# Batch 0's scores in two banks, the embeddings' place, the routing's arithmetic, and the planner's clock

## The chip, the cores and the metric

The kernel runs on one core of a Trainium2 chip. The metric is the device time of one execution in microseconds; the median of three runs is given. A core has TensorE (PE, matrix products; PEld is its weight load), VectorE (DVE), ScalarE (ACT), GpSimd (POOL) and SyncE (SP, which here only issues transfers). Each takes its instructions in the order in which they were put into its queue.

## The reference

Three layers follow one another. `x` is 8 batches x 8 heads x 512 x 64, `state` 8 x 8 x 32 x 64; there are 8 x (512 + 32) = 4608 tokens of 512 numbers, in 36 tiles of 128.

```python
a = softmax(x @ state.T / 8);  xread = a @ state          # per batch and head
a2 = softmax(state @ x.T / 8); sread = a2 @ x
x = concat([xread, sread])                                # 4608 x 512 tokens
x = square(maximum(x @ w_in, 0)) @ w_out                  # 512 -> 2048 -> 512
xn = x / (norm(x) + 1e-6); en = emb / (norm(emb) + 1e-6)
logits = xn @ en.T / tau                                  # 8 experts
e = argmax(logits); gate = softmax(logits)[e]
out = gate * (maximum(x @ w1[e], 0) @ w2[e])              # 512 -> 1024 -> 512
```

## The kernel before

Nearly all products are made of float16 pairs: a number is split into a high and a low half, and a product is three float16 products (high x high, high x low, low x high). The weights of the first dense layer arrive as 64-bit numbers, in 16 blocks (8 of `w_in`, 8 of `w_out`); ACT and DVE turn each into float32 bits (`to_f32`, lines 864 to 896: a scaling on ACT, line 882, and three integer steps on DVE, lines 885, 887 and 894), ACT squares it (lines 911, 967) for a scale, and both split it.

The order of all instructions is written before the kernel runs, by a planner in the same file (`Plan`, line 103). Each piece of work is a generator, a thread with a priority. It yields `(engine, duration)` before it issues instructions, or an event or a buffer ring to wait for. `run` (line 150) picks again and again the thread that can start earliest by the plan's own clock, the smaller priority number first, and lets it issue. So the durations that threads yield set only the order within the queues; on the chip, semaphores make each instruction wait for its inputs. `dma` (line 137) gives the plan's arrival time of a load. Everything else follows from these orders, so any edit of a duration or a priority can move instructions in all queues.

The stages run into one another. In the first 130 us the weights are prepared, batch 0 goes through attention and the first tokens through the dense layer in float32 (`first_attention` to `first_state_w`, lines 560 to 665; line 1412). Batches 1 to 7 follow (`attention`, line 448), with the dense layer in pairs (`up1`, `down1`, lines 1325 and 1367) and the routing of each tile. From about 700 us on the experts' layer runs (`moe2`, line 1773).

What the change touches:

- Batch 0's scores. `first_attention` takes one tile `S` of two PSUM banks; `first_scores(t)` (line 591) makes 16 float32 products for each half `t` as soon as that half of `x` is there; `weigher` (line 508) then makes the softmax of the half: maximum (line 519), subtraction (521), exponential on ACT (528), sum (530), normalisation (532 to 536), a float16 split (540, 542) and a turned read by DMA on SP's queue (549). `weights` (line 976) asks for the weight blocks from the fifth on only after both turned reads were asked for (`AHEAD`, `ev("asked", t)`).
- `embeddings` (line 1134) normalises the eight expert embeddings: 3 small DVE steps, a float32 product with ones (line 1146), 19 small DVE steps (1149 to 1159, with `rsqrt`). It waits for the weights' scale and for `prepare`, which loads `tsb` (tau) and `emf` (the embeddings) on SP's queue (lines 1817 to 1830).
- Routing. `route_tile` (line 1166) squares a finished tile, makes a power-of-two scale from the sum (`pow2`, line 294), splits, turns and multiplies with the embeddings. `route_group` (line 1205) works for four tiles at once (the last group has two): scale, largest logit, one-hot `oh`, and the running count `cum` of tokens per expert, one DVE addition per tile (line 1246); one product with a triangle of ones and one with ones of `cum` (lines 1253, 1254) give each token's place in its expert's list, to which the expert's base is added (1259).

Of the kernel before, what the change touches and what calls it, by code (L numbers as in the profile page):

```python
# [10 lines left out]
F32 = mybir.dt.float32  # L11
F16 = mybir.dt.float16
# [10 lines left out]
NE, FE = 8, 1024  # L23
# [34 lines left out]
RECS = 6  # L58
MARG = 1.75
# [43 lines left out]
class Plan:  # L103
# [10 lines left out]
    MARGIN = MARG  # L114

    def __init__(self):
        self.free = dict.fromkeys(("pe", "act", "dve", "pool", "sp"), 0.0)
        self.dma_free = 0.0
        self.threads = []
        self.cur = None  # L120
# [28 lines left out]

    def run(self):  # L150
        while self.threads:
            best = None
            for th in self.threads:
                r = th[3]
                if isinstance(r, Ev):
                    if r.time is not None:
                        th[2] = max(th[2], r.time)
                        self._advance(th)
                        break
                elif isinstance(r, Slots):  # L160
                    if r.ready():
                        th[2] = max(th[2], r.take())
                        self._advance(th)
                        break
                else:
                    dep = r[2] if len(r) > 2 else th[2]
                    if r[0] == "pe" and 1.3 <= th[1] < 5:
                        dep += self.MARGIN
                    key = (max(dep, self.free[r[0]]), th[1])
                    if best is None or key < best[0]:  # L170
                        best = (key, th, dep)
            else:
                assert best is not None, "threads wait for each other"
                (start, _), th, dep = best
                eng, dur = th[3][0], th[3][1]
                self.free[eng] = start + dur
                th[2] = start + dur + self.LAT
                self._advance(th)
# [57 lines left out]
def tiny(k):  # L236
    return "dve", TINY * k
# [7 lines left out]
def moe_kernel(  # L245
# [47 lines left out]

    def pow2(s, inv, v, K):

        m = small.tile([128, 4], F32, name="p2m")[:, :v.shape[1]]
        V.tensor_scalar(out=m.bitcast(I32), in0=v.bitcast(I32), scalar1=0x7F000000, scalar2=1,
                        op0=ALU.bitwise_and, op1=ALU.logical_shift_right)
        V.tensor_scalar(out=s.bitcast(I32), in0=m.bitcast(I32), scalar1=-1.0, scalar2=float(K << 23),
                        op0=ALU.mult, op1=ALU.add)  # L300
        V.tensor_scalar(out=inv.bitcast(I32), in0=m.bitcast(I32), scalar1=float((254 - K) << 23), scalar2=None,  # L301
                        op0=ALU.add)
# [74 lines left out]
    cum = const.tile([128, NT + 1, NE], F16, name="cum")  # L377
    nc.gpsimd.memset(cum[:, 0, :], 0.0)
# [21 lines left out]
    def ev(*key):  # L400
        return evs.setdefault(key, Ev(plan))
# [46 lines left out]
    def attention(b):  # L448
# [56 lines left out]
        w = weigher(b, Sp, xh, xl, scl, 0, 32)  # L505
        yield from w

    def weigher(b, Sp, xh, xl, scl, m0, m1):

        ms, n = slice(m0, m1), NS * (m1 - m0)  # L510
        S4 = Sp.rearrange("p a (h n) -> p (a h) n", n=NS)[:, ms]
# [10 lines left out]
        ev("S read", b, m1).set()  # L522
        if m1 == 32:
            if m0:
                yield ev("S read", b, m0)
            s_slots.release()
# [33 lines left out]
    def first_attention():  # L560

        yield ev("st", 0)
        stt = st_t.pop(0)
        yield xhl_slots
        xh, xl = halves_tile()
        ss = small.tile([128, 3], F32, name="ss")
        yield act(256)
        nc.scalar.activation(out=xl.bitcast(BF16)[:, :, :64], in_=stt, func=AF.Square, accum_out=ss[:, 2:3])
        yield t_slots
        p = ps_t.tile([128, 512], F32, name="t")  # L570
        yield "pe", 0.2
        mm(p[:, 2:3], lhsT=one32, rhs=ss[:, 2:3], start=True, stop=True)
        mm(p[:, 256:512], lhsT=oneb, rhs=xl.bitcast(BF16)[:, :, :64], start=True, stop=True)
        yield s_slots
        Sp = ps_s.tile([128, 4, 256], F32, name="S")
        for t in range(2):
            plan.add(first_scores(t, Sp, xh, xl, stt), 0.4 + 0.1 * t)
        plan.add(first_scale(ss, stt), 0.95)
        v = small.tile([128, 2], F32, name="sv")[:, 0:1]
        yield tiny(4)  # L580
        V.tensor_scalar(out=v, in0=p[:, 2:3], scalar1=FLOOR, scalar2=None, op0=ALU.max)
        pow2(sx[:, 1:2], isx[:, 1:2], v, 204)
        yield sth_slots
        sthl = att.tile([128, 2, 4, 64], F16, name="sthl")
        stf = sthl.rearrange("p a c n -> p (a c n)").bitcast(F32).rearrange("p (c n) -> p c n", c=4)
        yield dve2(256)
        V.tensor_scalar(out=stf, in0=stt, scalar1=sx[:, 1:2], scalar2=float(2.0 ** -14), op0=ALU.mult, op1=ALU.mult)
        plan.add(first_state_w(stf), 0.6)
        plan.add(group_bound(0, p), 0.7)

    def first_scores(t, Sp, xh, xl, stt):
        yield ev("first x", t)
        xf = xf_t[0, 0]
        yield "pe", 2.0
        for sb in (2 * t, 2 * t + 1):
            for c in range(4):
                mm(Sp[:, sb, c * 64:c * 64 + 64], lhsT=xf[:, c, sb * 128:sb * 128 + 128], rhs=stt[:, c, :],
                   start=True, stop=True)
        ev("scored", t).set()
        yield from weigher(0, Sp, xh, xl, eighth, 16 * t, 16 * t + 16)  # L600
# [533 lines left out]
    def embeddings():  # L1134
        yield ev("wo scale")
        yield ev("prepared")
        yield "dve", 3.0
        V.reciprocal(out=itau, in_=tsb)
        V.tensor_scalar(out=itau, in0=itau, scalar1=float(2.0 ** -14), scalar2=None, op0=ALU.mult)
# [7 lines left out]
        yield tiny(20)  # L1147
# [3 lines left out]
        y = small.tile([128, NE], F32, name="eny", bufs=1)  # L1151
        rsqrt(y, v, NE)
        V.tensor_tensor(out=y, in0=y, in1=v, op=ALU.mult)
# [12 lines left out]
    def route_tile(i, ps, k_h, rc, st):  # L1166
# [8 lines left out]
        yield tiny(4)  # L1175
        f2 = st["f2"][:, j:j + 1]
        V.tensor_scalar(out=f2, in0=f2, scalar1=FLOOR, scalar2=None, op0=ALU.max)
        s2 = small.tile([128, 1], F32, name="s2")
        pow2(s2, st["is2"][:, j:j + 1], f2, 204)
# [25 lines left out]
    def route_group(i0, m, recs, k_r, st):  # L1205
# [15 lines left out]
        yield tiny(12)  # L1221
        V.tensor_tensor(out=ui, in0=u1[:, i0:i0 + m], in1=is2, op=ALU.mult)
        rsqrt(y, f2, m)
        yield tiny(9)
        V.tensor_tensor(out=L, in0=f2, in1=y, op=ALU.mult)
        V.tensor_tensor(out=L, in0=L, in1=u1[:, i0:i0 + m], op=ALU.mult)
        V.tensor_scalar(out=L, in0=L, scalar1=1e-6, scalar2=None, op0=ALU.add)
# [4 lines left out]
        V.tensor_tensor(out=eq, in0=l2, in1=bc(lm), op=ALU.is_equal)  # L1232
# [224 lines left out]
    def list_of(which, J, tiles):  # L1457
# [7 lines left out]
        mm(pc[:, 0:NE], lhsT=one16, rhs=cum[:, tiles, :], start=True, stop=True)  # L1465
# [13 lines left out]
        V.tensor_copy(tot, pc[:, 0:NE])  # L1479
# [337 lines left out]
    def prepare():  # L1817

        yield ev("w_in asked")
        yield from load(cs, cst, 1 << 17)  # L1820
        yield from load(cs16, cst16, 1 << 16)
        yield from load(rid, rowid, 1 << 15)
        yield from load(tsb, tau.to_broadcast([128, 1]), 512)
        t = yield from load(emf, embT, 1 << 14)
        yield "pool", 1.0, t
        dz = mg.tile([128, REC], F32, name="rec0", bufs=1)
        nc.gpsimd.memset(dz, 0.0)
        nc.gpsimd.tensor_copy(dz[:, 513:514].bitcast(I32), rid[:, NT:NT + 1])
        yield from load(rec_d[NOREC:NOREC + 1, :], dz[0:1, :].bitcast(I32), 2048)
        ev("prepared").set()  # L1830

    def start():
        plan.add(first_attention(), PRIO_A0)
        yield from load_st(0)
# [7 lines left out]
        plan.add(embeddings(), 3)  # L1842
# [50 lines left out]
```

## Time and profile before

| | |
|---|---|
| median of 3 runs | 1088.94 us (1087.68 to 1089.35) |
| the profiled execution | 1089.88 us, span 1088.1 us from the first to the last instruction |
| mean granted clock of PE | 0.984 |
| PE busy | 1039.9 us (96% of the span), 10657 products |
| DVE busy | 684.6 us (63%) |
| ACT busy | 588.2 us (54%) |
| POOL busy | 124.3 us (11%) |
| DMA | 211.74 MB, mean 195 GB/s |

Busy times are shares of the span. [...] In a row of the timeline the part in brackets is the time for which the engine stood idle just before, and what ended it. In a row of waits stand who waited, for whom, the total, the number of times and the longest.

### The profile page before, as it was taken

How to read it: one execution, taken by the hardware profiler on the slowest of the kernel's cores; microseconds unless marked ns; L12 is line 12 of the kernel's file. 1: busy time of each engine (PE TensorE's matmuls, PEld its weight loads, DVE VectorE, ACT ScalarE, POOL GpSimd, SP SyncE). 2: the span in 40 equal slices, each digit the busy share in tenths (PEclk: the TensorE clock that was granted, in tenths of full speed). 3: DMA queues.
4: the chain of work that ended last, by engine and by line, in shares of the span. 5: the costliest groups of instructions: out<-in, count | busy, mean ns of one | idle time of the engine just before them, and what ended most of it. 6: DMA issues, size and time to landing. Idle time of an engine off the chain costs nothing. (4 is left out here: it accounts for less than half of the span.)

```text
span 1088.1 us, 26339 instructions
## 1 busy us (share of the span) xinstructions
PE 1039.9 (96%) x10657; PEld 672.2 (62%) x10657; DVE 684.6 (63%) x1787; ACT 588.2 (54%) x976; POOL 124.3 (11%) x149
## 2 busy tenths in 40 slices
PE   4679999999999999999999999999999999999997
PEld 3345446565656566565555666677677777767774
DVE  5788798868878778887797784466322323222222
ACT  4778779787887988887787984211110101111110
POOL 0000000200101001002002020312122121212111
PEclk8799999999999999999999999999999999999999
DMA  6873144874875565887559587753898777694691
GB/s 216 288 248 110 60 97 146 233 209 133 242 226 150 153 181 173 233 210 217 166 162 262 194 262 246 218 138 80 277 285 166 195 226 219 169 292 141 182 311 69
DMA packets 161311, 211.74 MB, mean 195 GB/s; under 512 B 112225, under 2 KB 114529, under 8 KB 155938
## 3 DMA queue, kind: packets, MB, share of 16 engines
q1 hardware_dynamic: 152866, 182.94, 58.2%
q0 software_dynamic: 8320, 27.08, 8.2%
q8 instruction: 85, 1.39, 0.5%
q14 instruction: 40, 0.33, 0.1%
HBM read 257.92 MB, written 51.68 MB: 285 GB/s over the span
## 5 line engine op out<-in xcount | busy, mean ns | idle before, releaser
L1699 ACT ACTIVATE r<-u 128x512 f32<-128x512 f32 x70 | 41.8, 597 | 319.5 <-PE u L1745 288.7
L1433 PE MATMUL d<-wo_t,g 128*128 128x512 f16 x480 | 182.1, 379 | 1.0 <-DVE g L1319 1.0
L1435 PE MATMUL d<-wo_t,g 128*128 128x512 f16 x480 | 182.1, 379 | 0.2
L1434 PE MATMUL d<-wo_t,g 128*128 128x512 f16 x480 | 182.1, 379 | 0.0
L1349 PE MATMUL u<-aT,sw 128*128 128x256 f16 x512 | 141.3, 276 | 9.7 <-ACT r L1302 7.6
L1351 PE MATMUL u<-aT,sw 128*128 128x256 f16 x512 | 141.0, 275 | 0.2 <-DVE sw L316 0.2
L1350 PE MATMUL u<-aT,sw 128*128 128x256 f16 x512 | 141.0, 275 | 0.0
L1702 DVE CAST hh<-r 128x512 f16<-128x512 f32 x70 | 29.9, 428 | 127.8 <-ACT r L1699 126.3
L1302 ACT ACTIVATE r<-u,cg 128x512 f32<-128x512 f32 x120 | 81.5, 680 | 47.9 <-PE u L1351 27.2
L1713 DVE TENSOR_SCALAR o<-d,rec,wo_t 128x512 f32<-128x512 f32 x35 | 28.3, 810 | 111.0 <-PE d L1768 108.5
L1275 POOL DMA_INDIRECT rec_d<-rec,pi x34 | 38.5, 1132 | 519.9 <-DVE is L301 140.8
L1768 PEld LDWEIGHTS <-hh 128*128 128x128 f16 (+1 forms) x688 | 54.7, 103 | 57.6 <-issue 1.3
L1321 DVE TENSOR_TENSOR g<-r,g 128x512 f16<-128x512 f32 x120 | 82.2, 688 | 7.5 <-ACT r L1316 5.9
L1435 PEld LDWEIGHTS <-g 128*128 128x128 f16 x480 | 46.9, 98 | 57.7 <-DVE g L1321 1.2
L1743 PE MATMUL u<-xes,stage 128*128 128x128 f16 x448 | 75.9, 219 | 0.0
L1745 PE MATMUL u<-xes,stage 128*128 128x128 f16 x448 | 75.9, 219 | 0.0
L1744 PE MATMUL u<-xes,stage 128*128 128x128 f16 x448 | 75.9, 219 | 0.0
L1433 PEld LDWEIGHTS <-g 128*128 128x128 f16 x480 | 47.2, 98 | 46.3 <-DVE g L1319 1.9
L1316 ACT ACTIVATE r<-r 128x512 f32<-128x512 f32 x120 | 74.5, 626 | 1.4
L1434 PEld LDWEIGHTS <-g 128*128 128x128 f16 x480 | 46.9, 98 | 44.2
L1743 PE MATMUL u<-xes,xx 128*128 128x128 f16 x416 | 70.5, 220 | 0.0
L1744 PE MATMUL u<-xes,xx 128*128 128x128 f16 x416 | 70.4, 219 | 0.0
(338 smaller groups left out, 2637.7 us busy)
## 6 DMA issues: line engine op xcount, KB each, us to landing
w_d<-he SPq DMA_DIRECT2D x128, 256.0 KB
g<-w_d SPq DMA_DIRECT2D x16, 2048.0 KB
wo_t<-w_d SPq DMA_DIRECT2D x16, 2048.0 KB
stage<-w_d SPq DMA_DIRECT2D x14, 2048.0 KB
he<-w_d SPq DMA_DIRECT2D x14, 2048.0 KB
xx<-w_d SPq DMA_DIRECT2D x13, 2048.0 KB
sw<-w_d SPq DMA_DIRECT2D x13, 2048.0 KB
stage<-in_w_dram SPq DMA_DIRECT2D x20, 1024.0 KB
```

Of the source, the lines that this page charges most:

```text
L1302: nc.scalar.activation(out=r, in_=ps, func=AF.Relu, scale=cg[:, g:g + 1] if u >= F32U else cgq[:, c:c + 1])
L1316: nc.scalar.activation(out=r, in_=r, func=AF.Square)
L1321: V.tensor_tensor(out=gl, in0=r, in1=gh, op=ALU.subtract)
L1349: mm(o, lhsT=hl[:, i, 0, fs], rhs=aT[:, i, :], start=i == 0, stop=False)
L1350: mm(o, lhsT=hl[:, i, 0, fs], rhs=aT[:, 2 + i, :], start=False, stop=False)
L1351: mm(o, lhsT=hl[:, i, 1, fs], rhs=aT[:, i, :], start=False, stop=i == 1)
L1433: mm(ps, lhsT=g_h[:, f, ts], rhs=w[:, 0, :], start=f == 0, stop=False)
L1434: mm(ps, lhsT=g_h[:, f, ts], rhs=w[:, 1, :], start=False, stop=False)
L1435: mm(ps, lhsT=g_l[:, f, ts], rhs=w[:, 0, :], start=False, stop=f == KF - 1)
L1743: mm(p[:, j, xs], lhsT=w[:, 0, k, fs], rhs=xe[:, k, xs], start=k == 0, stop=False)
L1744: mm(p[:, j, xs], lhsT=w[:, 0, k, fs], rhs=xe[:, 4 + k, xs], start=False, stop=False)
L1745: mm(p[:, j, xs], lhsT=w[:, 1, k, fs], rhs=xe[:, k, xs], start=False, stop=k == 3)
```

## The change

The plan's clock: PE's durations pass through `slowed`. The plan's time is cut into equal stretches; in a stretch PE counts at half speed unless the one before was used for enough of its length. The first load counts as arriving 1.2 us later. Batch 0's scores: each half gets a PSUM bank of its own, from the ring of the dense layer's `u` tiles, and gives it back once its half is read; `weigher` gets a function to call for that. PE gets five products of ones with ones (`warm`) at the start and four more ahead of the scores. The embeddings' two loads go to ACT's queue, and `embeddings` is started at once, with priority 0.9 instead of 3, in smaller pieces. Routing: the clamp and the inverse scale are made once per group instead of once per tile, steps are fused, the counts of a group are one reduction over `tally` (a ring of four groups, which holds each group's starting counts and its one-hots; 36 times the expert's number is put into the first group's starting counts, so that the product with ones carries the base); the product with ones becomes one per tile of the group. `pow2` is cut into `half`, `power` and `inverse` with the same arithmetic; `list_of` takes the base off again.

```diff
+TALLY = 4
...
-        self.dma_free = 0.0
+        self.dma_free = 1.2
+        self.windows = {}
...
+    def slowed(self, start, dur):
+
+        t, left = start, dur
+        while left > 1e-9:
+            w = int(t / self.WINDOW)
+            before = self.windows.get(w - 1, (0.0, 0.5))
...
+            step = min(left / rate, (w + 1) * self.WINDOW - t + 1e-6)
+            self.windows[w] = self.windows.get(w, (0.0, rate))[0] + step, rate
+            t, left = t + step, left - step * rate
+        return t - start
...
+                if eng == "pe":
+                    dur = self.slowed(start, dur)
...
-        ev("S read", b, m1).set()
-        if m1 == 32:
-            if m0:
-                yield ev("S read", b, m0)
-            s_slots.release()
+        read()
...
+        yield d_slots
+        idle, k_d = ps_d.tile([128, 512], F32, name="d"), d_slots.last()
+
+        def warm(n):
+            yield "pe", 0.25 * n
+            for _ in range(n):
+                mm(idle.rearrange("p (a n) -> p a n", a=4), lhsT=oneb, rhs=oneb.unsqueeze(1).to_broadcast([128, 4, 128]),
+                   start=True, stop=True)
+
+        yield from warm(5)
...
-        yield s_slots
-        Sp = ps_s.tile([128, 4, 256], F32, name="S")
+        at = plan.now()
+        yield from warm(4)
+        d_slots.release(k_d)
+        plan.cur[2] = at
         for t in range(2):
-            plan.add(first_scores(t, Sp, xh, xl, stt), 0.4 + 0.1 * t)
-        plan.add(first_scale(ss, stt), 0.95)
+            plan.add(first_scores(t, xh, xl, stt), 0.4 + 0.1 * t)
+        plan.add(first_scale(ss, stt), 1.2)
...
-    def first_scores(t, Sp, xh, xl, stt):
+    def first_scores(t, xh, xl, stt):
         yield ev("first x", t)
         xf = xf_t[0, 0]
-        yield "pe", 2.0
-        for sb in (2 * t, 2 * t + 1):
+        at = plan.now()
+        yield u_slots
+        plan.cur[2] = max(at, plan.now())
+        Sp, k_h = ps_u.tile([128, 512], F32, name="u").rearrange("p (a n) -> p a n", a=2), u_slots.last()
+        yield "pe", 1.9
+        for a in range(2):
+            sb = 2 * t + a
             for c in range(4):
-                mm(Sp[:, sb, c * 64:c * 64 + 64], lhsT=xf[:, c, sb * 128:sb * 128 + 128], rhs=stt[:, c, :],
+                mm(Sp[:, a, c * 64:c * 64 + 64], lhsT=xf[:, c, sb * 128:sb * 128 + 128], rhs=stt[:, c, :],
                    start=True, stop=True)
         ev("scored", t).set()
-        yield from weigher(0, Sp, xh, xl, eighth, 16 * t, 16 * t + 16)
+        S4 = Sp.rearrange("p a (h n) -> p (a h) n", n=NS)
+        yield from weigher(0, S4, xh, xl, eighth, 16 * t, 16 * t + 16, lambda: u_slots.release(k_h))
...
-        yield ev("wo scale")
-        yield ev("prepared")
-        yield "dve", 3.0
+        yield "act", 1.0
+        nc.scalar.dma_start(emf, embT)
+        nc.scalar.dma_start(tsb, tau.to_broadcast([128, 1]))
+        plan.cur[2] += 2.5
+        yield tiny(1)
         V.reciprocal(out=itau, in_=tsb)
+        yield tiny(2)
...
-        yield tiny(4)
-        f2 = st["f2"][:, j:j + 1]
-        V.tensor_scalar(out=f2, in0=f2, scalar1=FLOOR, scalar2=None, op0=ALU.max)
+        yield tiny(2)
         s2 = small.tile([128, 1], F32, name="s2")
-        pow2(s2, st["is2"][:, j:j + 1], f2, 204)
+        half(st["is2"][:, j:j + 1], st["f2"][:, j:j + 1])
+        power(s2, st["is2"][:, j:j + 1], 204)
...
-        yield tiny(12)
-        V.tensor_tensor(out=ui, in0=u1[:, i0:i0 + m], in1=is2, op=ALU.mult)
+        g, u1s = i0 // 4, u1[:, i0:i0 + m]
+        yield tiny(14)
+        inverse(is2, is2, 204)
+        V.tensor_tensor(out=ui, in0=u1s, in1=is2, op=ALU.mult)
+        V.tensor_scalar(out=f2, in0=f2, scalar1=FLOOR, scalar2=None, op0=ALU.max)
         rsqrt(y, f2, m)
-        yield tiny(9)
+        yield tiny(7)
         V.tensor_tensor(out=L, in0=f2, in1=y, op=ALU.mult)
-        V.tensor_tensor(out=L, in0=L, in1=u1[:, i0:i0 + m], op=ALU.mult)
-        V.tensor_scalar(out=L, in0=L, scalar1=1e-6, scalar2=None, op0=ALU.add)
+        if g < B:
+            V.tensor_scalar(out=L, in0=L, scalar1=u1s[:, 0:1], scalar2=1e-6, op0=ALU.mult, op1=ALU.add)
+        else:
+            V.tensor_tensor(out=L, in0=L, in1=u1s, op=ALU.mult)
+            V.tensor_scalar(out=L, in0=L, scalar1=1e-6, scalar2=None, op0=ALU.add)
...
-        V.tensor_tensor(out=eq, in0=l2, in1=bc(lm), op=ALU.is_equal)
...
-        oh = small.tile([128, 4, NE], F16, name="oh")[:, :m]
-        yield tiny(3 + m) + (at,)
-        V.tensor_tensor(out=eq, in0=eq, in1=revb, op=ALU.mult)
+        if g >= TALLY:
+            yield ev("ranked", g - TALLY)
+        turn_ = tally[:, g % TALLY]
+        oh = turn_[:, 1:1 + m, :]
+        yield tiny(4) + (at,)
+        V.scalar_tensor_tensor(out=eq, in0=l2, scalar=0.0, in1=revb, op0=ALU.is_equal, op1=ALU.mult)
         V.tensor_reduce(out=em, in_=eq, axis=X, op=ALU.max)
         V.tensor_tensor(out=oh, in0=revb, in1=bc(em), op=ALU.is_equal)
-        for j in range(m):
-            V.tensor_tensor(out=cum[:, i0 + j + 1, :], in0=cum[:, i0 + j, :], in1=oh[:, j, :], op=ALU.add)
+        if i0 == 0:
+            V.tensor_scalar(out=turn_[:, 0, :], in0=eix, scalar1=float(NTOK // 128), scalar2=None, op0=ALU.mult)
+        at = plan.now()
+        if i0 + m < NT:
+            after = tally[:, (g + 1) % TALLY, 0, :]
+            if g + 1 >= TALLY:
+                yield ev("ranked", g + 1 - TALLY)
+        else:
+            after = seen[:, 1, :]
+        yield tiny(1) + (at,)
+        with nc.allow_low_precision("counts up to 272"):
+            V.tensor_reduce(out=after, in_=turn_[:, 0:m + 1, :].rearrange("p a e -> p e a"), axis=X, op=ALU.add)
+        if i0 + m == SEEN:
+            V.tensor_copy(seen[:, 0, :], after)
...
-        yield "pe", 0.06
+        yield "pe", 0.15
         mm(pk[:, 0:m * NE], lhsT=ltri16, rhs=oh.rearrange("p a e -> p (a e)"), start=True, stop=False)
-        mm(pk[:, 0:m * NE], lhsT=one16, rhs=cum[:, i0:i0 + m, :].rearrange("p a e -> p (a e)"), start=False, stop=True)
+        for j in range(m):
+            mm(pk[:, j * NE:m * NE], lhsT=one16, rhs=turn_[:, 0:m - j, :].rearrange("p a e -> p (a e)"), start=False,
+               stop=j == m - 1)
+        ev("ranked", g).set()
...
-        yield tiny(4)
-        V.tensor_tensor(out=po, in0=pk[:, 0:m * NE].rearrange("p (a e) -> p a e", a=m),
-                        in1=cs[:, C_EB:C_EB + NE].unsqueeze(1).to_broadcast([128, m, NE]), op=ALU.add)
+        yield tiny(3)
+        V.tensor_tensor(out=po, in0=pk[:, 0:m * NE].rearrange("p (a e) -> p a e", a=m), in1=oh, op=ALU.mult)
         t_slots.release()
-        V.tensor_tensor(out=po, in0=po, in1=oh, op=ALU.mult)
...
-        mm(pc[:, 0:NE], lhsT=one16, rhs=cum[:, tiles, :], start=True, stop=True)
+        mm(pc[:, 0:NE], lhsT=one16, rhs=seen[:, 0 if tiles == SEEN else 1, :], start=True, stop=True)
...
-        yield from load(tsb, tau.to_broadcast([128, 1]), 512)
-        t = yield from load(emf, embT, 1 << 14)
-        yield "pool", 1.0, t
+        t = plan.now()
+        yield "pool", 1.0, t + 2.0
...
+        plan.add(embeddings(), 0.9)
...
-        plan.add(embeddings(), 3)
```

## Rows read from the trace of the kernel before

**Rows 1.** Windows: length; busy PE, PEld, DVE, ACT, POOL; PEclk; DMA share, GB/s.

```profile
0.00:130.00 130.00, 96.91 (x605) 55.10 (x606) 98.81 (x209) 92.98 (x136) 3.69 (x17) 0.87 0.57 193
...
0.00:12.60 12.60, 7.85 (x37) 7.50 (x39) 2.15 (x12) 1.79 (x3) 1.23 (x10) 1.00 0.84 288
12.60:50.00 37.40, 18.32 (x138) 9.62 (x138) 31.58 (x56) 29.06 (x39) 0.18 (x1) 0.72 0.76 266
...
130.00:1082.60 952.60, 942.98 (x10053) 617.13 (x10051) 585.01 (x1578) 495.25 (x840) 119.65 (x131) 1.00 0.69 196
1082.60:1088.10 5.50, 0.02 (x1) 0.00 (x0) 0.81 (x1) 0.00 (x0) 0.97 (x1) 0.90 0.14 51
```

**Rows 2.** Windows in which the granted clock is at its lower level.

```profile
18.20:35.60 17.40, 7.51 (x57) 3.89 (x57) 15.11 (x26) 12.11 (x16) 0.00 (x0) 0.51 0.64 197
46.00:52.60 6.60, 5.65 (x41) 2.56 (x42) 5.63 (x15) 6.60 (x10) 2.47 (x7) 0.50 0.29 115
80.00:86.90 6.90, 4.78 (x22) 3.30 (x23) 6.74 (x16) 5.34 (x9) 0.00 (x0) 0.51 0.25 73
117.60:121.00 3.40, 3.40 (x5) 1.31 (x4) 3.06 (x13) 3.37 (x6) 0.00 (x0) 0.50 0.40 77
```

**Rows 3.** Waits from 0 to 120 us: total us, times, longest us.

```profile
PE u L919 <- ACT pjk L911: 16.6, 5, 5.5
...
PE t L467 <- ACT xx L461: 4.9, 1, 4.9
...
ACT r L1302 <- PE u L1351: 4.5, 5, 1.6
...
DVE wv L925 <- PE u L919: 3.2, 3, 2.0
```

**Rows 4.** Timeline, 0 to 16 us: start us, duration us, instruction, idle before and releaser.

```profile
0.77 0.41 SPq L338 DMA_DIRECT2D stt<-in_stT_dram  x1
...
2.93 0.42 ACT L568 ACTIVATE xx<-stt 128x256 bf16<-128x256 f32 x1 [0.89 <-DMA stt<-in_stT_dram]
...
5.54 7.06 PE L597 MATMUL S<-stt,xx 128*128 128x64 f32 x32 [1.17 <-DMA xx<-in_xT_dram]
...
12.64 0.69 DVE L519 TENSOR_REDUCE mx<-S 128x16 f32<-128x512 f32 x1 [5.84 <-PE S L597]
...
14.15 0.72 ACT L528 ACTIVATE xx<-xx,eighth 128x512 f32<-128x512 f32 x1 [10.72 <-DVE xx L521]
```

**Rows 5.** Timeline, 20 to 47 us: SP's queue and POOL's first use of row numbers.

```profile
20.97 5.08 SPq L549 DMA_TRANSPOSE aT<-xx  x2
...
26.09 1.16 SPq L338 DMA_DIRECT2D g<-in_w_in_dram  x2
...
39.10 0.43 SPq L338 DMA_DIRECT2D rid<-in_rowid_dram  x1
...
46.96 0.18 POOL L1828 COPY rec<-rid 128x1 int32<-128x1 int32 x1 [45.18 <-DMA rid<-in_rowid_dram]
```

**Rows 6.** Timeline, 109 to 123 us: the embeddings on DVE and PE.

```profile
109.10 0.15 DVE L1138 RECIPROCAL itau<-tsb 128x1 f32<-128x1 f32 x1
...
113.92 0.96 PE L1146 MATMUL t<-emq,one 128*128 128x8 f32 x8
...
118.97 0.15 DVE L1149 TENSOR_SCALAR env<-t 128x8 f32<-128x8 f32 x1
...
122.67 0.19 DVE L1159 TENSOR_TENSOR en_l<-emq,en_h 128x32 f16<-128x32 f32 x1
```

**Rows 7.** Timeline of PE, 168 to 171 us.

```profile
168.09 0.38 PE L1433 MATMUL d<-wo_t,g 128*128 128x512 f16 x1
168.30 0.38 PE L1434 MATMUL d<-wo_t,g 128*128 128x512 f16 x1
...
170.04 0.17 PE L1196 MATMUL t<-en_h,xr 128*128 128x8 f16 x1
...
170.31 0.17 PE L1198 MATMUL t<-en_h,xr 128*128 128x8 f16 x1
```

More of the change, by code (lines that the diff above doesn't have):

```diff
@@ L114 @@
     MARGIN = MARG
+    WINDOW = 3.413
     def __init__(self):
         self.free = dict.fromkeys(("pe", "act", "dve", "pool", "sp"), 0.0)
-        self.dma_free = 0.0
+        self.dma_free = 1.2
+        self.windows = {}
         self.threads = []
@@ L148, in _advance @@
         self.cur = was
+    def slowed(self, start, dur):
[3 more added lines that the diff above has]
+            before = self.windows.get(w - 1, (0.0, 0.5))
+            rate = 1.0 if before[0] > (0.75 if before[1] < 1 else 0.45) * self.WINDOW else 0.5
+            step = min(left / rate, (w + 1) * self.WINDOW - t + 1e-6)
+            self.windows[w] = self.windows.get(w, (0.0, rate))[0] + step, rate
+            t, left = t + step, left - step * rate
+        return t - start
     def run(self):
@@ L291, in moe_kernel, with half, power, inverse @@
     FLOOR = float(2.0 ** -100)
+    def half(m, v):
+        V.tensor_scalar(out=m.bitcast(I32), in0=v.bitcast(I32), scalar1=0x7F000000, scalar2=1,
+                        op0=ALU.bitwise_and, op1=ALU.logical_shift_right)
+    def power(s, m, K):
+        V.tensor_scalar(out=s.bitcast(I32), in0=m.bitcast(I32), scalar1=-1.0, scalar2=float(K << 23),
+                        op0=ALU.mult, op1=ALU.add)
+    def inverse(inv, m, K):
+        V.tensor_scalar(out=inv.bitcast(I32), in0=m.bitcast(I32), scalar1=float((254 - K) << 23), scalar2=None,
+                        op0=ALU.add)
     def pow2(s, inv, v, K):
         m = small.tile([128, 4], F32, name="p2m")[:, :v.shape[1]]
[L297 to L302, printed above, removed]
+        half(m, v)
+        power(s, m, K)
+        inverse(inv, m, K)
     def rsqrt(y, v, n):
@@ L376, in moe_kernel @@
     en_l = const.tile([128, 4, NE], F16, name="en_l")
-    cum = const.tile([128, NT + 1, NE], F16, name="cum")
-    nc.gpsimd.memset(cum[:, 0, :], 0.0)
+    tally = const.tile([128, TALLY, 5, NE], F16, name="tally")
+    seen = const.tile([128, 2, NE], F16, name="seen")
     wi_t = mwi.tile([128, NB, 2, 4, BW], F16, name="wi")
@@ L504, in attention, with weigher @@
                     mm(o, lhsT=w[:, c, ss_], rhs=a[:, c, :], start=n == 0, stop=n == 2)
-        w = weigher(b, Sp, xh, xl, scl, 0, 32)
-        yield from w
-    def weigher(b, Sp, xh, xl, scl, m0, m1):
+        S4 = Sp.rearrange("p a (h n) -> p (a h) n", n=NS)
+        yield from weigher(b, S4, xh, xl, scl, 0, 32, s_slots.release)
+    def weigher(b, S4, xh, xl, scl, m0, m1, read):
         ms, n = slice(m0, m1), NS * (m1 - m0)
-        S4 = Sp.rearrange("p a (h n) -> p (a h) n", n=NS)[:, ms]
         mx = small.tile([128, 32], F32, name="mx")[:, ms]
@@ L589, in first_attention @@
         plan.add(group_bound(0, p), 0.7)
-    def first_scores(t, Sp, xh, xl, stt):
+    def first_scores(t, xh, xl, stt):
         yield ev("first x", t)
         xf = xf_t[0, 0]
-        yield "pe", 2.0
-        for sb in (2 * t, 2 * t + 1):
+        at = plan.now()
[5 more added lines that the diff above has]
+            sb = 2 * t + a
             for c in range(4):
-                mm(Sp[:, sb, c * 64:c * 64 + 64], lhsT=xf[:, c, sb * 128:sb * 128 + 128], rhs=stt[:, c, :],
+                mm(Sp[:, a, c * 64:c * 64 + 64], lhsT=xf[:, c, sb * 128:sb * 128 + 128], rhs=stt[:, c, :],
                    start=True, stop=True)
         ev("scored", t).set()
-        yield from weigher(0, Sp, xh, xl, eighth, 16 * t, 16 * t + 16)
+        S4 = Sp.rearrange("p a (h n) -> p (a h) n", n=NS)
+        yield from weigher(0, S4, xh, xl, eighth, 16 * t, 16 * t + 16, lambda: u_slots.release(k_h))
     def first_scale(ss, stt):
@@ L1146, in embeddings @@
             mm(p[:, 0:NE], lhsT=one32, rhs=e2[:, k, :], start=k == 0, stop=k == 3)
-        yield tiny(20)
+        yield tiny(1)
         v = small.tile([128, NE], F32, name="env", bufs=1)
@@ L1151, in embeddings @@
         y = small.tile([128, NE], F32, name="eny", bufs=1)
+        yield tiny(5)
+        yield tiny(6)
         rsqrt(y, v, NE)
+        yield tiny(4)
+        yield tiny(4)
         V.tensor_tensor(out=y, in0=y, in1=v, op=ALU.mult)
@@ L1478, in list_of @@
         yield tiny(12)
-        V.tensor_copy(tot, pc[:, 0:NE])
+        V.tensor_tensor(out=tot, in0=pc[:, 0:NE], in1=cs[:, C_EB:C_EB + NE], op=ALU.subtract)
         t_slots.release()
```

## The prediction

> **What bounds the kernel now.** I read the table of stages first. TensorE (PE) is busy for 96.91 of the first 130 us and for 942.98 of the next 952.6; after it ends only a tail of 5.5 us is left [rows 1]. So the kernel has two parts. From 130 us on PE is the bound: work that leaves VectorE (DVE) or ScalarE (ACT) there is worth at most a part of the 9.6 us that PE still idles. Before 130 us PE idles 33.1 us, and what it does is partly done at the lower of its two clock levels. In that part a time is won whenever PE's work is fed earlier.
>
> [...]
>
> Then I read who ends the waits. PE waits 16.6 us in five pieces on ACT's squares of the first-layer weights and 4.9 us in one piece on ACT's squares for batch 1. The other way round, ACT waits 4.5 us and DVE 3.2 us on a PE that comes late [rows 3]. ACT and DVE feed the front: between 12.6 and 50 us DVE is busy 31.58 of 37.4 us, ACT 29.06 [rows 1]. So I price the front as a queue of DVE and ACT work: an earlier start or less work there passes on to PE, as long as the loads keep up.
>
> Last I read the start in order of time. The 32 score products of batch 0 (line 597) run from 5.54 us for 7.06 us. DVE has nothing for 5.84 us and makes its first reduction of the scores at 12.64; ACT idles 10.72 us until its first exponential at 14.15 [rows 4]. The two turned reads of batch 0 are issued from 20.97 us, and the next weight load behind them on SP's queue only at 26.09 [rows 5].
>
> **The change, part by part.**
>
> A. Two banks for the scores. The first reduction reads only the first 16 products, yet waits for all 32. Half of 7.06 is 3.53 us, so alone it could start near 5.54 + 3.53 = 9.1. But two things now stand before the scores in PE's queue. I followed the planner's rules by hand to see the order: the embeddings' product becomes ready in the plan at about 4.4 us, the warm-ups just behind, the scores at 5.1; all three end up in that order. The embeddings' product took 0.96 us [rows 6]. A 512-column product takes the step of 0.21 us from one start to the next, so four warm-ups cost 0.86 us [rows 7]. Against these 1.82 us stands PE's idle 1.17 us before the first score [rows 4]: the scores begin 0.65 us later, at 6.2, the first half is done at 9.7, the second at 13.2. DVE's heavy work then starts 2.9 us earlier. The second half's chain starts no earlier, but it no longer queues behind the first half's five large DVE steps, so the turned reads and the loads behind them should also come some 3 us earlier. Bounds: nothing, if the loads between 26 and 47 us hold the front anyway; 5.1 us, if both turns are out by the time the first now is (26.09 - 20.97) [rows 5]. I take 2.9, the shift of the row nearest to the edit.
>
> The first five warm-ups fall where PE waits for ACT's first square, which ends at 3.35 us [rows 4]; they cost nothing. Without that cover they would cost 5 x 0.215 = 1.1 us. What they give is nothing either by the rows: the clock is full there without them.
>
> [...]
>
> B. Embeddings early. 3 + 19 small DVE steps leave the stretch from 109.10 to 122.86: three of some 0.15 us and a block of 3.89 us, together 4.3, and the product of 0.96 us leaves PE at 113.92 [rows 6]. In their new place DVE has the idle 5.84 us as cover, apart from the three that now wait for the two small loads. Those loads move from SP's to ACT's queue; one issue takes 0.43 us on SP [rows 5], two 0.86, and ACT idles 0.89 us before its first square at 2.93 [rows 4], so that is covered too; uncovered, it delays the start by up to 0.9 us. SP gets 0.9 us back at 39 us, where it does not bind. The gain: at most 4.3 us, if DVE feeds PE directly there; at least nothing, because PE is busy when the block ends, and the lead has to live on until a later idle of PE. All of those after 130 us are 9.6 us [rows 1]. Also in the stretch is the fourth slow window, worth 1.7 us [rows 2]. I take 1.5.
>
> C. The plan's clock, its DMA start and the priorities. No instruction is added by these; the order in the queues changes, in all five, mostly in the front, because only there does the plan see idle PE. The rows show what order can give: ACT's and DVE's waits on a late PE, 4.5 + 3.2 = 7.7 us [rows 3], are of the kind that a plan with a slower PE foresees. And what one stall costs either way: the 4.9 us wait, with the slow window of 80 to 86.9 us behind it (4.78 / 2 = 2.4), 7.3 us [rows 2, 3]. Bounds: -15 and +7.3. I take -1.5, a fifth of the 7.7, since a list of priorities does not remove most waits.
>
> D. Shorter routing. A group of four tiles loses three clampings, three inverses, one fused pair in the scale, one in the comparison, three of the four count steps and the base's addition: 12 DVE steps, at 0.15 to 0.19 us each [rows 6] about 2 us, 16 us for all nine groups. It lies after 112 us, nearly all of it where PE is the bound: worth nothing, at most a part of the 9.6 us. PE gets 3 more products in eight groups and one in the last: 25. Twelve small products start within 0.27 us, 0.025 apart [rows 7]: 0.6 us, on PE, so on the path. If each cost its whole 0.17 us it would be 4.2. I take 0.6, the stepping of a row of the same kind.
>
> The sum: -2.9 - 1.5 - 1.5 + 0.6 = -5.3 us. The profiled execution took 1089.88 us (span 1088.1 and 1.8 around it), 0.94 above the median of the three runs, 1088.94. So 1084.6 in a profile, 1083.6 as a median.
>
> **The rivals.**
>
> 1. The new order pays more. One stall like the 4.9 us one goes together with its slow window: 7.3 instead of the 1.5 in C, so 1077.8. [...] Against: the waits have several causes, the largest group (16.6 us) is PE waiting for ACT's throughput, which no order mends.
>
> 2. Nothing moves. The lead of A is lost while the weights load, B's lead finds PE busy, C is a wash: 1088.94 + 0.6 = 1089.5, or 1088.5 with a microsecond left of A. For it: PE is busy all through when the embeddings' block ends. Against: DMA is busy only 0.76 of the time from 12.6 to 50 us [rows 1], it is held up by the turns that A brings forward. That DVE still waits for both halves in spite of two banks comes out here as well: A and its 2.9 us go, 1086.5.
>
> 3. Slower by order. The queues are fixed, so a new order can put a product before PE's ready work whose input is late, as at 80 us. One new stall of that kind, with the slow window behind it, costs 7.3: 1088.94 - 2.9 - 1.5 + 0.6 + 7.3 = 1092.4. It decides from the point where the stall exceeds the 3.8 us that A and B bring less D. For it: the whole front is ordered anew. Against: the plan's PE comes closer to the slow windows that the rows show.
>
> 4. The embeddings' loads land late. DVE's first steps and PE's product before the scores wait for them. The small load of row numbers, issued at 39.10 while other loads ran, was first used at 46.96 [rows 5], 7.9 us; the small load of the state came within 2.2 us [rows 4]. In the first case they land at 9.1, scores start at 10.9, the first half is read at 14.4 (1.8 late), the second is done at 18 (5.3 late): 1088.94 + 1.8 to 5.3 less 2.4 from B to D, 1088.3 to 1091.8. It decides from a landing at 7.3 (12.64 less 3.53, 0.96 and 0.86). I go by the state's row: it too is loaded before the queue is full. [...]
>
> [...]
>
> **Chances.** Forecast 0.45 (its own range 1080 to 1087), rival 1 0.17, rival 2 0.16, rival 3 0.12, rival 4 0.07, rival 5 0.03. A difference of 0.2%, 2.2 us, is about what a measurement of this kernel tells from no change: faster is below 1086.8, slower above 1091.1. Faster: 0.42 + 0.17 + 0.02 + 0.01 + 0.03 = 0.65. The same: 0.03 of the forecast, 0.14 of rival 2, 0.03 each of rivals 3 and 4, 0.23. Slower: 0.09 + 0.03 = 0.12. The range runs from 1075, between rival 1 and the lower bound of C, to 1092.5, where rival 3 stands.
>
> **What would show it.** A: the first reduction of the scores near 9.7 instead of 12.64 and the load now at 26.09 near 23. B: no DVE block at 119 us; the embeddings' product before 5.5 us. C: fewer than 16.6 + 4.9 us of waits on ACT, less busy time at 0.50. D: DVE's total down by about 16 us, PE's work at full clock up by 0.6. In all, PE's idle in the first 130 us down from 33.1 to about 28, with the stretch after it unchanged. The prediction is wrong if that idle does not fall, or if PE's waits after 130 us grow beyond 9.6.

## The result, and the profile after

The changed kernel takes 1097.65 us (median of 17 runs, 1095.4 to 1100.35), the kernel before beside it 1091.41 (17 runs, 1087.68 to 1095.36). The ratio is 1.0056, with a 95% interval of 1.0043 to 1.0069: 6.2 us slower, where 5.3 us faster was forecast. Its profiled execution took 1095.44 us, with a span of 1093.7. One of c1's six executions below (3991.71 us) and one of c2's (1214.06 us) were in a slow state and are left out of the ratios.

The stages of the changed kernel, in the columns of [rows 1]:

```profile
0.00:130.00 130.00, 98.15 (x661) 56.24 (x662) 103.78 (x215) 95.72 (x141) 6.25 (x16) 0.93 0.57 194
0.00:12.60 12.60, 10.55 (x40) 7.71 (x41) 4.82 (x28) 3.46 (x5) 1.19 (x9) 1.00 0.79 259
12.60:50.00 37.40, 22.01 (x106) 11.74 (x106) 32.05 (x58) 26.45 (x36) 1.23 (x1) 0.95 0.70 245
130.00:1088.00 958.00, 946.77 (x10031) 618.88 (x10029) 568.32 (x1469) 494.80 (x840) 118.24 (x131) 1.00 0.70 194
```

TensorE (PE) idles 31.85 us before 130 us, not the 28 that were forecast (33.1 before), and 4.2 us of what counts as busy are the nine warm-ups. After 130 us it idles 11.2 us (9.6 before), which the prediction named as a sign that it is wrong. VectorE (DVE) lost 11.7 us of work in all (684.6 to 672.9 by the profile's page), and no gain in time can be seen from it. By the time of single products most of the loss is there early: the first fp16 down product starts at 166.1 us (161.2 before), the first expert product at 710.8 (705.8), the last at 1088.0 (1082.2).

Over the whole span PE idles as long as before: 1093.7 - 1045.3 = 48.4 us, against 1088.1 - 1039.9 = 48.2. What has grown in this pair of profiles is its busy time, by 5.4 us:

```profile
PE 1045.3 (96%) x10691; PEld 675.1 (62%) x10691; DVE 672.9 (62%) x1684; ACT 590.5 (54%) x980; POOL 125.5 (11%) x148
```

The nine warm-ups are 4.2 us of it, and the embeddings' product takes 1.87 instead of 0.96. Five of the warm-ups (2.3 us) stand where PE idled before, so elsewhere it idles that much more.

The start, in order of time, beside [rows 4]:

```profile
1.30 2.32 PE L589 MATMUL d<-oneb 128*128 128x512 bf16 x5 [1.30 <-POOL eighth L381]
...
4.58 0.16 DVE L1179 RECIPROCAL itau<-tsb 128x1 f32<-128x1 f32 x1 [4.58 <-DMA tsb<-in_tau_dram]
...
5.09 1.87 PE L1188 MATMUL t<-emq,one 128*128 128x8 f32 x8 [0.75 <-DVE emq L1183]
...
6.82 1.87 PE L589 MATMUL d<-oneb 128*128 128x512 bf16 x4
...
8.48 6.93 PE L635 MATMUL u<-stt,xx 128*128 128x64 f32 x32
```

The scores start at 8.48, 2.9 us later than before. The first half is read at 12.03, only 0.6 us earlier, and the second at 15.44 (13.97). What follows on SP's queue, beside [rows 5], is late too, by 1.9 us:

```profile
22.85 5.08 SPq L570 DMA_TRANSPOSE aT<-xx  x2
27.98 1.16 SPq L364 DMA_DIRECT2D g<-in_w_in_dram  x2
```

The largest waits of PE from 50 to 170 us (total us, times, longest), first of the kernel before and then of the changed one. One long stall is gone, another has come:

```profile
PE t L467 <- ACT xx L461: 4.9, 1, 4.9
PE u L1349 <- ACT r L1302: 2.6, 3, 1.8
PE u L919 <- ACT pjk L911: 1.9, 1, 1.9
PE d L1412 <- DVE rec L316: 1.8, 1, 1.8
```

```profile
PE d L1478 <- DVE rec L342: 5.8, 1, 5.8
PE u L1415 <- ACT r L1368: 3.3, 4, 1.0
PE u L1415 <- ACT sw L698: 2.4, 1, 2.4
PE u L958 <- ACT pjk L950: 2.0, 2, 1.0
```

That stall can be followed back through the queues. The square of the last block of weights on ScalarE (ACT), which closes the weights' scale, and the scale itself on DVE (the step that writes `unit`), before:

```profile
100.17 1.13 ACT L967 ACTIVATE pjk<-stage 128x1024 bf16<-128x1024 f32 x1
...
105.97 0.21 DVE L995 SCALAR_TENSOR_TENSOR ends<-ends 128x1 f32<-128x1 f32 x1
...
116.66 2.00 PE L1412 MATMUL d<-wo_t,g 128*128 128x512 f32 x3 [1.79 <-DVE rec L316]
```

and after:

```profile
109.19 1.14 ACT L1006 ACTIVATE pjk<-stage 128x1024 bf16<-128x1024 f32 x1
...
116.66 0.21 DVE L1034 SCALAR_TENSOR_TENSOR ends<-ends 128x1 f32<-128x1 f32 x1
...
121.86 5.77 PE L1478 MATMUL d<-wo_t,g 128*128 128x512 f32 x8 [5.76 <-DVE rec L342]
```

The block had been asked for at 86.51 (84.05 before). DVE finished the square's input at 103.3 (99.6 before); then, in ACT's new order, the square stands behind batch 1's two splits of x and several splits of weights. So 3.7 us of the delay come from DVE's order, 5.3 from ACT's, and 1.7 from the steps between the square and the scale. The first tiles can't be scaled before 116.66, their banks come free late, and PE's next products wait.

### The profile page after: what moved, and what is told of

The parts are those of the page before. It is cut to its first block, busy times and chain, and to the rows that moved or that the text cites. A ratio compares the mean times of both kernels' runs of the same rounds, so it can differ in the third digit from the quotient of the medians.

```text
span 1093.7 us, 26305 instructions
## 1 busy us (share of the span) xinstructions
PE 1045.3 (96%) x10691; PEld 675.1 (62%) x10691; DVE 672.9 (62%) x1684; ACT 590.5 (54%) x980; POOL 125.5 (11%) x148
## 5 line engine op out<-in xcount | busy, mean ns | idle before, releaser
L1415 PE MATMUL u<-aT,sw 128*128 128x256 f16 x512 | 141.2, 276 | 15.7 <-ACT r L1368 9.9
L1415 PEld LDWEIGHTS <-sw 128*128 128x128 f16 x512 | 51.6, 101 | 32.6 <-issue 13.8
L1809 PE MATMUL u<-xes,xx 128*128 128x128 f16 x416 | 70.5, 219 | 0.0
```

Of the source, the lines that this page charges most:

```text
L1415: mm(o, lhsT=hl[:, i, 0, fs], rhs=aT[:, i, :], start=i == 0, stop=False)
L1809: mm(p[:, j, xs], lhsT=w[:, 0, k, fs], rhs=xe[:, k, xs], start=k == 0, stop=False)
```

## Experiments

Ratios are to the kernel before, timed beside it on the same chip, and the numbers in brackets are 95% intervals; beside the e and r runs that kernel took 1103.8 us, beside the c and d runs 1089 to 1090. Each run left one trace, and times within an execution are from that one. "In before's order" means that only instructions were edited and the generators' yields left as they were, so that the planner sees no difference. Two theories at first: the instructions ahead of the scores cost the time, or the new order of the queues does.

**e1, the changed kernel without its nine warm-up products** (their plan price stays, so the order does):

```diff
             yield "pe", 0.25 * n
-            for _ in range(n):
-                mm(idle..., lhsT=oneb, rhs=oneb..., start=True, stop=True)
```

> The changed kernel without its nine warm-up products; the plan still counts their time, so every queue keeps its order. The changed kernel stands at a ratio of 1.0056 to the kernel before. Theory 1 (start): the products ahead of batch 0's scores run at half clock and delay everything behind them; the scores then start 1.9 us earlier (6.6 instead of 8.5) and the ratio falls by 0.0017 to about 1.004. Theory 2 (order): what is lost is lost by the new order in the queues further on; the ratio stays at 1.0056.

Ratio 1.0085 [1.0065, 1.0105]; the changed kernel itself where the kernel before takes as long (r5) 1.0093 [1.0059, 1.0127], a little above its expected range. The ratios can't tell 1.7 us from nothing, the traces can: the scores start at 6.8 instead of 8.5 and the first fp16 down product at 164.6 (166.3 in r5), but the last one at 719.5 (718.7). The lead is lost behind the front.

> The changed kernel once more, on the chip of the three kernels beside it: ratio 1.0043 to 1.0069 as measured; higher, up to 1.0085, if the loss grows on a chip on which all kernels are slower.

**e2, the kernel before with 5 + 10 warm-ups that the plan doesn't see:**

```diff
+        warm(5)
         yield ev("st", 0)
...
         mm(p[:, 256:512], lhsT=oneb, rhs=xl.bitcast(BF16)[:, :, :64], start=True, stop=True)
+        warm(10)
```

> The kernel before with 5 + 10 warm-up products that the plan does not see, so its order is kept; the scores of batch 0 start near 8.6 instead of 5.5 us, as in the changed kernel. Theory 1 (start): the delay of 3 us passes on to the end, ratio 1.0028. Theory 2 (order): the front has slack that swallows it, ratio 1.0000 to 1.0005.

Ratio 0.9981 [0.9966, 0.9996], the only interval wholly below 1. Neither theory expected a gain; but one interval among some fifteen that misses 1 by 0.0004 can be chance. Its timeline of PE:

```profile
4.12 3.73 PE L566 MATMUL d<-oneb 128*128 128x512 bf16 x10
7.69 3.68 PE L606 MATMUL S<-stt,xx 128*128 128x64 f32 x32
11.30 1.94 PE L759 MATMUL t<-xx,stt 128*64 128x512 f32 x8
```

The 32 scores take 3.68 us, half of the 7.06 of [rows 4]. So by their spacing, 0.22 us against 0.11, they ran at the lower clock level before, though the granted clock reads 1.00 there [rows 1].

**e3 and e4, the plan's clock alone.** e3 takes it out of the changed kernel, e4 puts it alone into the kernel before:

```diff
 # e3
-                if eng == "pe":
-                    dur = self.slowed(start, dur)
...
-        self.dma_free = 1.2
+        self.dma_free = 0.0
 # e4: the same lines, the other way, and slowed()
```

> The changed kernel with the plan's PE at full speed and its first load at 0 again; all instructions stay, the order changes. Theory 2 (order): the loss goes, ratio 1.000 or below. Theory 1 (start): the early embeddings and the warm-ups stay ahead of the scores, ratio 1.003 or more.

> The kernel before with nothing changed but the plan's clock and its first load at 1.2 us: the same instructions in another order. Theory 2 (order): slower, ratio 1.003 to 1.0056. Theory 1 (start): ratio 1.000 within 0.002.

e3: 1.0082 [1.0059, 1.0105]. The loss did not go, as the theory of the order had expected: priorities and yields of the change are still in it, so its order is a third one and not that of before. e4, with the same instructions as before: 1.0288 [1.0265, 1.0311]. The order alone can cost five times what the change cost. In e4 the first fp16 down product starts at 161.6, about as early as before; most of the loss comes later. PE idles 15 us between 500 and 700 us and 7.6 between 700 and 1000, where r2 and r3 below, in before's order and where the kernel before takes as long, idle 1.3 to 2.7 and 3.5 to 4.4:

```profile
500.00:700.00 200.00, 185.00 (x1506) 113.24 (x1505) 144.63 (x413) 149.63 (x249) 18.87 (x23) 0.97 0.67 201
700.00:1000.00 300.00, 292.44 (x3633) 210.93 (x3632) 109.41 (x339) 39.99 (x70) 57.46 (x56) 0.99 0.67 194
```

**r3, r2, c3 and r1, the edits in before's order:** the two banks, the routing, the embeddings, and all of them with the nine warm-ups.

```diff
 # r3
-        Sp = ps_s.tile([128, 4, 256], F32, name="S")
+        Sps = [ps_u.tile([128, 512], F32, name="u")... for _ in range(2)]
 # r2: half/power/inverse, tally and seen as in the change
 # c3
-        yield from load(tsb, ...); t = yield from load(emf, ...)
+        nc.scalar.dma_start(emf, embT); nc.scalar.dma_start(tsb, ...)   # at the start
...
         mm(p[:, 256:512], lhsT=oneb, ...)
+        emb = emb_first()        # reciprocal, squares, product
...
+        emb_rest(*emb)           # the other steps, in batch 0's softmax
```

> The kernel before with batch 0's score halves in two banks alone, in the order of before. The first reduction of the scores should start near 9.1 instead of 12.6 us. If an earlier start passes on: -2 to -3.5 us, ratio 0.997 to 0.998. If the queues behind it, which keep their order, swallow it: 1.000.

> The kernel before with the short routing alone, in the order of before. The prediction's price: 25 more products, +0.6 us, and 16 us of VectorE work less where TensorE is the bound, ratio 1.0000 to 1.0006. If VectorE's relief counts: down to 0.997.

> Before's queue order, only the embeddings moved to the start: their product ahead of the scores, their seven steps of VectorE in batch 0's softmax. If this is what costs the instruction edits their +0.3% (1.0032 all together, 0.9987 and 1.0001 the two others alone): 1.002 to 1.005, scores from about 7.1 instead of 5.46 at 0.22 us apart, turned scores read at 22.5 to 23.5 (before 20.97). Rival, the embeddings cost nothing at the start and the warm-ups did: 0.999 to 1.001.

> All the instruction edits of the change (two banks, nine warm-ups, early embeddings with their product ahead of the scores, short routing), but every thread still yields what it yielded before, so the queues keep the order of the kernel before. Theory 2 (the order costs, not the instructions): ratio 0.998 to 1.001. Theory 1 (the instructions cost, at the start above all): ratio 1.004 to 1.006, like the changed kernel.

Banks 0.9987 [0.9967, 1.0008], routing 1.0001 [0.9982, 1.0019], embeddings 1.0006 [0.998, 1.0033], all 1.0032 [1.0012, 1.0052]. PE's and DVE's timeline with the banks alone:

```profile
5.46 7.06 PE L597 MATMUL u<-stt,xx 128*128 128x64 f32 x32 [1.10 <-DMA xx<-in_xT_dram]
...
9.15 0.69 DVE L519 TENSOR_REDUCE mx<-u 128x16 f32<-128x512 f32 x1 [2.36 <-PE u L597]
```

The first half is read at 9.15, and the turned reads are asked for at 18.57 instead of 20.97. In r1, with the embeddings' product and the warm-ups in front, these are 12.38 and 21.55. r1 lies between the ranges of the two theories. r3's interval holds both a gain of 2.9 us and none. c3 (scores at 6.63) costs nothing that can be measured, where 1.002 to 1.005 was expected, though its interval reaches 1.0033. No single edit is shown to carry r1's 0.3%.

**c1 and c2, banks and warm-ups together in before's order:** r3 with `warm(5)` and then `warm(10)` (c1) or `warm(5)` (c2), put in as in e2.

> Before's queue order, with batch 0's score halves in two banks and 5 + 10 warm-up products ahead of the scores. If the two gains stand beside each other (banks alone 0.9987, warm-ups alone 0.9981): 0.996 to 0.9975; scores from 7.7 us at 0.11 us apart, first half read at about 9.8, turned scores read at 18 to 18.6 (before 20.97). Rival, the queue behind gives every gain at the start back: 0.998 to 1.0 although the turned scores are read 2 us earlier.

> As the run with 5 + 10 warm-ups, with 5 of the 10 taken away. If what lifts the clock is dense bf16 work up to the scores, the first scores start at about 5.9 and most run 0.22 us apart, as in the changed kernel, and the first half is read at about 9.5; ratio 0.998 to 0.9995. Rival, five are enough: scores from 5.9 at 0.11 us apart, first half read at 7.9, ratio under 0.997.

c1: 0.9983 [0.9959, 1.0007]; c2: 1.0004 [0.9977, 1.003]. In c1's trace the turned reads are asked for at 17.8 (20.97 before), the last fp32 down product starts at 149.1 (152.1), the last fp16 one at 703.2 (705.2), and the last expert product at 1082.6 (1082.2). The lead of 3.2 us is given back on the way: the rival. In c2 the turned reads are asked for even earlier, at 17.0, and of that lead of 4.0 us 3.6 are left at the first fp16 down product (157.6), 2.2 at the last (703.0) and 1.0 at the end of the span (1087.1). Its 32 scores start at 6.25 and take 4.25 us, between the two cases of the expectation; the first half is read at 8.75.

**r4 and d1, one number of the plan.** The price of a small DVE step, in the kernel before (r4) and in the changed one (d1):

```diff
-TINY = 0.18
+TINY = 0.19
```

> Before's instructions, with the plan's price of a small VectorE step at 0.19 us instead of 0.18, and so another queue order. If before's order is a picked one and any new order loses: 1.004 or more, with PE's added idle time anywhere in the span. Rival, only counting TensorE at half clock made the order worse: 0.998 to 1.002.

> The changed kernel with the plan's price of a small VectorE step at 0.19 us instead of 0.18: the same instructions in another queue order. If the changed kernel's order is one draw among many, as the same edit of the kernel before showed for its order (1.0242), the ratio lands away from the changed kernel's 1.0056 to 1.0093 by over 0.3%, on either side, and its added idle of TensorE stands at another place than the 5.8 us at 121.9 us. Rival, the edits fix the loss whatever the order: 1.005 to 1.010 again.

r4: 1.0242 [1.0214, 1.0269]; d1: 1.0109 [1.0068, 1.015]. Nothing of the change is in r4. It idles 13.4 us between 700 and 1000 us, where the kernel before idles 1.2; the waits of PE from 120 us on show where:

```profile
PE u L1743 <- DMA xes<-rec: 7.2, 1, 7.2
PE u L1349 <- ACT r L1302: 4.5, 5, 2.4
...
PE u L1743 <- DMA stage<-w_d: 2.8, 1, 2.8
```

At the step from the shared layer to the experts, the experts' first gathers and weights come late. d1's stall of the first tiles stayed (6.3 us at 121.8), against its expectation; it lost more behind, with 14.9 us of idle PE from 300 to 1000 us (8.9 in d3, the changed kernel beside it). Its four times, 1101.59 to 1103.92, all lie above the nine of d3, 1094.12 to 1100.56, though the intervals of the ratios overlap.

**d2, the stall taken away:** the last block of weights goes ahead in the changed kernel's plan. d3 is the changed kernel beside it.

```diff
-        plan.add((wi_block if kind == "i" else wo_block)(n, q), PRIO_W + 0.02 * n)
+        plan.add((...)(n, q), 0.3 if n == len(BLOCKS) - 1 else PRIO_W + 0.02 * n)
```

> The changed kernel with the last block of weights ahead of the others in the plan, so that ScalarE squares it right behind the block before it and not behind batch 1's splits. If its square at 109.2 us (before 100.2) is what costs the changed kernel its 5 us: the weights' scale is known by 104 to 108 us (116.7), the stall of 5.8 us at L1478 falls under 2 us, its products end by 154 us (158.7), and the ratio falls by 0.3 to 0.5% against the changed kernel, to 1.000 to 1.005. Rival, another stall takes its place as the order behind is drawn anew: the scale early, the ratio at 1.006 or more.

> The changed kernel itself, beside the two edits of it on the same chip: 1.0056 to 1.0093 by either theory; it is the measure for the other two.

d2: 1.0116 [1.0075, 1.0157]; d3: 1.006 [1.0038, 1.0082]. ACT, DVE and PE of d2, at the places shown above:

```profile
94.27 1.18 ACT L1006 ACTIVATE pjk<-stage 128x1024 bf16<-128x1024 f32 x1 [0.29 <-DVE stage L926]
...
103.51 0.21 DVE L1034 SCALAR_TENSOR_TENSOR ends<-ends 128x1 f32<-128x1 f32 x1
...
117.86 1.55 PE L1478 MATMUL d<-wo_t,g 128*128 128x512 f32 x3 [1.05 <-DVE rec L342]
```

The mechanism is as read: the square at 94.3 instead of 109.2, the scale 13 us earlier, the stall 1.05 instead of 5.76 us, and the last fp32 down product starts at 149.9 (158.7 in the changed kernel, 152.1 before). Up to 2.6 us of these leads can have another source: most of d2's scores ran at the higher level by their durations, 275 ns against 421 (last section), and its turned reads were asked for at 20.26, not 22.87 as in d3. Yet the kernel ends later than the changed one, as the rival has it: its four times, 1102.47 to 1104.25, all lie above the nine of d3. The stages behind show where the lead went:

```profile
300.00:500.00 200.00, 194.93 (x1704) 114.87 (x1703) 160.94 (x412) 166.23 (x286) 15.84 (x24) 1.00 0.66 191
500.00:700.00 200.00, 196.01 (x1606) 122.10 (x1605) 139.35 (x396) 139.70 (x234) 13.34 (x17) 1.00 0.64 193
700.00:1000.00 300.00, 293.37 (x3896) 215.20 (x3895) 104.00 (x291) 35.21 (x61) 63.56 (x62) 0.99 0.68 200
```

PE idles 5.1 + 4.0 + 6.6 = 15.7 us in these three, against 3.4 + 1.4 + 4.1 = 8.9 in d3, 3.4 + 1.8 + 2.1 = 7.3 in the first profile of the changed kernel and 1.5 + 0.8 + 1.2 = 3.5 before.

**Together.** Seven kernels keep before's order: 0.9981 to 1.0032. Seven have one of six other orders, the changed kernel among them: 1.0056 to 1.0288, whether they hold all of the change, none of it or a part. Order and edits both cost. Beside each other on one chip the medians are 1103.75 us (before), 1107.76 (r1, all the edits in before's order) and 1112.80 (r5, the changed kernel): about 4 us for the edits (1.3 to 5.7 by the interval of r1) and 5 for the order. In the traces PE is busy equally long in r1 and r5 (1051.3 and 1050.5 us) and idles 3.8 us more in r5 (59.4 and 55.6). How the 6.2 us of the first pair divide was not measured.

## Why the prediction was wrong

Both halves of the sum failed. A, B and D together forecast -3.8 us, and the edits in before's order cost +4.0 (r1); C forecast -1.5, and the new order cost +5.0 (r5 less r1).

**A, two banks (-2.9 us): the first step that failed, by the price of what stands ahead and by the path to the end.** By itself the split did at the start what was worked out: half of 7.06 after the scores' start is 9.1, measured 9.15, and what follows was 2.4 us earlier at the turned reads (r3). But the 1.82 us for the products ahead of the scores were full-clock prices: the granted clock reads 1.00 around [rows 6] (113 to 115 us) and [rows 7] (168 to 171 us). From the start of the embeddings' product to the scores it took 8.48 - 5.09 = 3.39 us, and that product started only at 5.09, behind tau's load at 4.58. The scores start at 8.48 where 6.2 was forecast, the first read is at 12.03 and not 9.7, and the turned reads come 1.9 us later than before, not 3 earlier. I had taken the row of the granted clock, 1.00 at the start [rows 1], for the level. The products say otherwise: PE's very first five take 2.32 us, some 0.43 apart, where products of 512 columns start 0.21 apart in [rows 7], and e2's scores run at twice the rate of before (32 in 3.68 us against 7.06). With the change's four warm-ups ahead, behind the embeddings' product, the scores of this trace step at 0.22 us as before (32 in 6.93 us).

Nor did a lead pass on to the end where there was one: c2's of 4.0 us at the turned reads gives a ratio of 1.0004.

**B, the embeddings (-1.5): no gain seen.** The moves are all there. The loads landed by 4.58, so rival 4 fell, and no block of DVE stands at 119 us any more. But the product is now ahead of the scores, and its DVE steps stand in batch 0's softmax. c3's ratio, 1.0006 [0.998, 1.0033], can't tell -1.5 us from nothing. In its trace scores and turned reads come 1.1 us late (6.63 and 22.04), and the first fp16 down product still 0.8 (162.0): what the late stretch gave back is some 0.3 us.

**C, the plan's order (-1.5, bounds -15 and +7.3): the second step that failed.** I took a part of the waits that a better informed plan would remove, and no account of the waits that it would make. "No instruction is added by these" was true. The waits that C named did shrink: up to 120 us PE waits 13.9 us on ACT's squares of the first-layer weights (16.6 before), and the 4.9 us on those of batch 1 are gone. Others took their place: rival 3's new stall came, at 121.9 us, 5.8 us long, with the clock down around it (0.72 from 117 to 122 us, 0.62 from 122 to 127.4). Rival 3's own terms, 7.3 and 0.6, come near the measured +6.2, but that is partly luck: it had no cost for the edits, and in the profile PE's idle time in sum has not grown. Its chance of 0.12 was too low, for all six other orders were slower than before's. The bound was wrong too: e4 and r4 put the cost of an order alone at 2.4 to 2.9%, some 26 to 32 us, four times my upper bound. The waits of [rows 3] were the wrong place to read that bound from: they say what an order still costs, not what it saves already. That the order before idles only 3.5 us in the 700 us from 300 to 1000 could have been a sign that it is hard to better.

**D, the routing (+0.6): not contradicted.** r2 is 1.0001, with 2 us of interval on either side; DVE's work fell by 10.9 us in r2 (684.6 to 673.7), where 16 were counted, and no change in time can be seen.

**What stays open.** r1's 0.3% has no single edit behind it (0.9987, 1.0001 and 1.0006 for the parts); its nine warm-ups alone were not run in before's order, and the intervals leave room for a sum of small ones. Where the leads of c1, c2 and e1 are lost between 160 us and the end was not followed. And why a better model of PE's clock doesn't give a better order: six orders show that they differ and that each loses at its own place, not what a good one has in common.

## What to carry to other kernels

In a kernel whose queues come from a list planner, first ask what an order costs: change one price in the plan by some per cent and time it. If that alone moves the time by more than the edit can bring, test the edit in the old order, and don't judge it by the new draw. And a stall that a trace shows plainly may be followed back correctly, removed, and still be worth nothing, when its removal draws a new order for all that comes behind.

## What the runs showed of the hardware

In the two profiles the granted clock's row is no reading of the level before its first fall. In the changed kernel it says 1.00 up to 44 us, and yet the products with 256 columns start 0.21 us apart at 37 us (PE's timeline), twice the 0.11 of the same products at 108.77 to 109.21, where it says 1.00 too. In the kernel before the same products start 0.21 us apart from 33.66 to 35.36, where the clock reads 0.51, and 0.11 apart from 35.76 on, where it reads 0.99 (35.6 to 46 us). The changed kernel:

```profile
37.00 0.42 PE L1415 MATMUL u<-aT,sw 128*128 128x256 f16 x1
37.22 0.42 PE L1416 MATMUL u<-aT,sw 128*128 128x256 f16 x1
37.43 0.42 PE L1417 MATMUL u<-aT,sw 128*128 128x256 f16 x1
...
108.77 0.27 PE L1415 MATMUL u<-aT,sw 128*128 128x256 f16 x1
108.88 0.27 PE L1416 MATMUL u<-aT,sw 128*128 128x256 f16 x1
```

The mean clocks of the two profiles can't be compared for that reason.

When the level rises at the start, by the durations of the scores, differs from trace to trace with the same products ahead. d2's products up to the scores are those of the changed kernel, and its scores start 0.2 us earlier. Here is the line of the scores in the changed kernel and then in d2 (shortest, median and longest duration in ns, first and last start in us):

```profile
L635 PE MATMUL u<-stt,xx x32: 314/421/421, 8.5 to 15.0; 128*128 128x64 f32 x32
L635 PE MATMUL u<-stt,xx x32: 275/275/421, 8.3 to 12.5; 128*128 128x64 f32 x32
```

In d2 most scores are short ones, and all 32 take about 4.5 us instead of 6.93. In r5 and d3, two more traces of the changed kernel itself, the line reads 314/421/421 and 314/421/422. So from one trace it can't be said with which products ahead the level rises; in e2 and c1, with 5 + 10 warm-ups ahead, all 32 scores took 3.68 us.
